# Linear attention and soft experts on one core: w's load moves to ScalarE's queue, the second expert product takes 384 columns at once, the last weight piece has one row

## Chip, cores and metric

The kernel runs on one core of a Trainium2 chip. The core has a matrix engine (PE, TensorE), a vector engine (DVE), a scalar engine (ACT), a general one (POOL, GpSimd), a sequencer that here only issues transfers (SP), and 16 DMA engines, which carry every transfer, whoever issues it. The metric is the device time of one execution, in microseconds (us); it is the median of several runs. The time before is 122.52 us, the median of three runs (122.45 to 122.78).

## What is computed

Two parts follow one another. First a recurrent linear attention with a decay `w` and a bonus `u` per head; then its output, seen as 3072 tokens of 384, goes through eight soft experts.

```python
batch, n_heads, seq, head_dim = (4, 8, 768, 48)     # r, k, v; w and u are (8, 48)
N, D, E, S_per_e, F = (3072, 384, 8, 4, 1024)       # phi (384, 32), w1 (8, 384, 1024), w2 (8, 1024, 384)

for t in range(S):                                   # attention, state is D x D for each head
    cur = einsum('bhd,bhe->bhde', u[None] * kt, vt)
    y[:, :, t] = einsum('bhd,bhde->bhe', rt, state + cur)
    state = w[None, :, :, None] * state + einsum('bhd,bhe->bhde', kt, vt)
...
logits = x @ phi
d = exp(logits - logits.max(0)); d /= d.sum(0) + 1e-09       # over tokens
slot_input = d.T @ x                                         # 32 slots, 4 for each expert
for e in range(E):
    h = maximum(slot_input[e] @ w1[e], 0.0)
    slot_out[e] = h @ w2[e]
c = exp(logits - logits.max(1)); c /= c.sum(1) + 1e-09       # over slots
out = c @ slot_out
```

All inputs and the output are float32. The inputs r, k and v are 4.7 MB each, w1 and w2 together 25 MB, the output 4.7 MB.

## The kernel before

**Order.** Every instruction is recorded through a helper that keeps the order of the program on its engine, so each engine runs its instructions exactly as they are written; what is left to the framework are the waits between engines and the space in memory. The framework puts a wait wherever one instruction needs what another wrote, or writes where another still reads. Transfers that SP and ACT issue share eight completion semaphores in turn, so such a transfer also waits until an earlier holder of its semaphore has landed.

**Start.** SP issues w as one row of 384 numbers (`w_row`, line 105), then k, r and v of batch 0, two heads at a time, then batches 1 and 2 and phi. ACT loads its function table (line 106) and issues two small transfers of w and u into `wu` (107, 108). PE runs four warm-up matmuls (line 144), then spreads `w_row` over the 128 partitions (line 177); ACT takes the logarithm (178), DVE multiplies by positions (188), ACT exponentiates (192), and with these powers of w, called W, k and r are scaled into `kr` (228): on DVE for the first pair of heads, on POOL for all others.

**Attention.** The sequence of each pair of heads is cut into two halves of three chunks of 128 steps; one half is one step i of the main loop (32 steps, with some steps ahead of it to fill the pipeline). PE transposes `kr`, makes the chunk products, and ACT and DVE move results out of PSUM. At step 3 SP issues batch 3 of k, r and v into the buffer that batch 0 used. Phi is turned to bfloat16 (`phi_b`, line 558) at step 5 and rearranged by PE at step 6. From step 13 on POOL issues the weights, each expert's matrix as one transfer that also turns float32 to bfloat16 (`load_w`, lines 135 and 138): eight of w1 and then eight of w2, these into buffers of k, r and v that are free by then. Ahead of the first of them POOL copies one column of batch 3's k (line 571). The last matrix, w2 of expert 7, comes in three pieces, of 4, 2 and 2 of its 8 rows `y` (line 576); a row is 128 partitions by 384 columns.

**Dispatch.** `acc` (32 slots by three blocks, and the sums) collects the slot inputs over the chunks; it is first written when the first half of batch 0 is done.

**Experts.** The slots of four experts share the 128 partitions, 32 for each, so there are two groups g of four. After w1 (line 623) and the transposes (648) comes `second` (660): for each row y, each half x of the 384 columns and each expert j, one matmul of 192 columns onto the partitions of that expert. Half 0 is summed in PSUM bank Xb, half 1 in bank Yb. Group 1 is run as experts 4 and 5, then 6, then 7, each as its weights arrive. Then `so`, the slot outputs in bfloat16, is written by DVE (half 0, line 671) and by ACT (half 1, line 672), both scaled by `csr`.

**Output.** 24 tiles of 128 tokens. For each, PE multiplies the weights of the slots with `so` (line 684), DVE or ACT scales the result into an output buffer (686, 688), and SP or POOL sends the buffers off in groups of 1, 1, 2, 2, 2, 4, 4, 4 and 4 tiles (line 704). The first two tiles are done in halves, left half on DVE, right half on ACT; the six PSUM banks used in turn are T1, T0, Ab, Vb, Xb, Yb.

Of the kernel before, what the change touches and what calls it, by code (L numbers as in the profile page):

```python
# [9 lines left out]
def kernel(  # L10
# [16 lines left out]
    Nn, Dm = out.shape  # L27
    ES = moe_phi.shape[1]
    E = moe_w1.shape[0]
    F = moe_w1.shape[2]  # L30
    Spe = ES // E
    nM = Dm // C
    nF = F // C
# [13 lines left out]
    bf = mybir.dt.bfloat16  # L47
    i32 = mybir.dt.int32
    AF = mybir.ActivationFunctionType
    ALU = mybir.AluOpType  # L50

    def O(ins):
        return tc.keep_in_program_order(ins)

    pe, dve, act, pool, sp = nc.tensor, nc.vector, nc.scalar, nc.gpsimd, nc.sync

    big = ctx.enter_context(tc.tile_pool(name="big", bufs=1))
    cst = ctx.enter_context(tc.tile_pool(name="cst", bufs=1))
# [6 lines left out]
    EG = E // 2  # L65
# [4 lines left out]
    def w2_of(e):  # L70
        g, j = divmod(e, EG)
        return raw[1 + g][:].bitcast(bf)[:, j * eW2:(j + 1) * eW2].rearrange("p (y d) -> p y d", y=nF)

    def raw_of(which, b):
        return raw[b % NR][:, which * RW:(which + 1) * RW]
# [5 lines left out]
    Yb = psb.tile([128, 512], f32, name="Yb")  # L81
    Xb = psb.tile([128, 512], f32, name="Xb")
# [12 lines left out]
    w_row = early[0:1, 0:H * D]  # L95
# [5 lines left out]
    phi_f = late[:, 128:128 + nM * ES]  # L101
    wu = cst.tile([8, 128], f32, name="wu")
    wu3 = wu[:].rearrange("q (e s) -> q e s", s=64)
    O(dve.memset(wu[:], 1.0))
    O(sp.dma_start(out=w_row, in_=w.rearrange("(o h) d -> o (h d)", o=1)))
    O(act.preload_act_table_set("natural_log_exp_and_others"))
    O(act.dma_start(out=wu3[0:4, :, 0:D], in_=w.rearrange("(q e) d -> q e d", e=2)))
    O(act.dma_start(out=wu3[4:8, :, 0:D], in_=u.rearrange("(q e) d -> q e d", e=2)))
# [104 lines left out]
    ones = cst.tile([128, 128], bf, name="ones")  # L213
    Le_t = [cst.tile([128, L, 128], bf, name=f"Le{j}") for j in range(2)]
    phi_s = cst.tile([128, nM, ES], bf, name="phi_s")
    phi_b = cst.tile([128, nM * ES], bf, name="phi_b")
    assert JV == nM
    acc = cst.tile([128, NA], f32, name="acc")
    guard = cst.tile([128, 1], f32, name="guard")
    st = {}  # L220

# [70 lines left out]
    def a_pe(i):  # L292
        m, b, q, g, n = at(i)
        kT, rT = st["kT", m], st["rT", m]
        for c in range(L):
            t = slice((g * L + c) * C, (g * L + c + 1) * C)
            for e in range(2):
                s = slice(64 * e, 64 * e + 64)
                O(pe.matmul(Ab[:, e, c * C:(c + 1) * C], kT[s, t], rT[s, t]))  # L299

    def mask_f(i):
        AT = wk.tile([128, 2, L, C], bf, name="AT", bufs=2)
        st["AT", i] = AT
        O(dve.tensor_mul(AT[:], Ab[:, :, 0:T].rearrange("p e (c t) -> p e c t", c=L),  # L304
                         mask_ut[:, None, None, :].to_broadcast([128, 2, L, C])))
# [112 lines left out]
    def disp(n, ds_p, first=True):  # L418
        x, Le = st["x", n], st["Le", n]
        for mi in range(nM):  # L420
            for c in range(L):
                O(pe.matmul(ds_p[:, mi * ES:(mi + 1) * ES].rearrange("p (j x) -> p j x", j=EG), x[:, c, mi:Dm:nM],
                            Le[:, c, :].rearrange("p (j x) -> p j x", x=32)[:, :, 0:2 * Spe],
                            start=(first and mi == 0 and c == 0), stop=(c == L - 1), skip_group_check=True))
        for c in range(L):
            O(pe.matmul(ds_p[:, NA - 1:NA], Le[:, c, :], ones[:, 0:1],
                        start=False, stop=(c == L - 1), skip_group_check=True))

    def disp_ev(n, ds_p):
        if n == 0:  # L430
            O(dve.tensor_copy(acc[:], ds_p))
        else:
            O(dve.tensor_add(acc[:], acc[:], ds_p))
# [37 lines left out]
    Wf = [t[:].rearrange("p q j d -> p (q j d)") for t in W]  # L471
# [3 lines left out]
    def turn(n, blocks, bank, eng):  # L475
        x, w_ = st["x", n], L * len(blocks) * C
        for b, mi in enumerate(blocks):
            for c in range(L):
                o = (b * L + c) * C
                O(pe.transpose(bank[:, o:o + C], x[:, c, mi * C:(mi + 1) * C], ident[:]))  # L480
        dst = xs[:, n - n0, blocks[0]:blocks[-1] + 1].rearrange("p m c t -> p (m c t)")
        if eng is dve:
            O(dve.tensor_copy(dst, bank[:, 0:w_]))
        else:
            O(act.copy(dst, bank[:, 0:w_]))
# [8 lines left out]
    for i in range(-5, nH):  # L494
        mu, odd = divmod(i, 2)
        if 0 <= i + 1 < nH:
            a_pe(i + 1)
            mask_f(i + 1)
        if pend:
            disp_ev(*pend.pop())  # L500
        if i == nH - 1:
            turn(n0, (2,), Vb[:].bitcast(bf), act)
            disp(n0 - 1, ds_t)
            le_t(n0 - 1)
            let_ev(n0 - 1, None, dve)
        if 0 <= i < nH:
            y_pe(i)
            y_evac(i)
        if 0 <= i + 2 < nH:
            v_pe(i + 2)  # L510
            v_evac(i + 2)
        if 0 <= i + 1 < nH:
            m_pe(i + 1)
            z_evac(i + 1)
        if odd == 0 and 0 <= mu + 1 < nU:
            prod_f(mu + 1)
        if odd and i > 0 and mu + 2 < nU:
            b_pe(mu + 2)
            b_evac(mu + 2)
        if odd and 0 <= mu + 3 < nU:  # L520
            scale(mu + 3, 0)
        if not odd and 0 <= mu + 2 < nU:
            scale(mu + 2, 1)
        route(i, 0)
        if 0 <= mu + 2 < nU:
            t_pe(mu + 2, odd)
            route(i, 1)
            t_evac(mu + 2, odd)
            if odd and i < 0:
                b_pe(mu + 2)  # L530
                b_evac(mu + 2)
        else:
            route(i, 1)
        if odd == 0 and 0 <= mu + 2 < nU:
            v_cast(mu + 2)
        route(i, 2)
        if i == nH - 3:
            turn(n0, (0, 1), T0, act)
        if i == nH - 2:
            turn(n1, (0, 1), T1, act)  # L540
        for f, j, q in T_AT.get(i, ()):
            f(j, q)
        if i in (-4, -3):
            wu_steps(i + 4)
        if i in Z_AT:
            q = Z_AT[i]
            O(act.activation(out=zt[:, q, 2, :], in_=zt[:, q, 0, :], func=AF.Copy, scale=wT[:, q:q + 1]))
        if i == 2:
            O(pool.memset(ones[:], 1.0))
            for t in Le_t:  # L550
                O(pool.memset(t[:], 0.0))
        if i == 3:
            load_kr(0, k, B - 1, 0, H)
            load_kr(1, r, B - 1, 0, H)
            for h0 in range(0, H, 2):
                load_v(B - 1, h0, h0 + 2)
        if i == 5:
            O(act.copy(phi_b[:], phi_f))
        if i == 6:
            for mi in range(nM):  # L560
                for j in range(nM):
                    o = C * mi - j + nM - 1
                    O(pe.matmul(Xb[:, mi * ES:(mi + 1) * ES].rearrange("p (j g s) -> p j g s", g=2, s=Spe),
                                Q3[:, o:o + C],
                                phi_b[:, j * ES:(j + 1) * ES].rearrange("p (g j s) -> p j g s", g=2, s=Spe),
                                start=(j == 0), stop=(j == nM - 1)))
            O(act.copy(phi_s[:].rearrange("p m s -> p (m s)"), Xb[:, 0:nM * ES]))
        if i == 28:
            O(pool.memset(uns, 0.0))
        if i == min(W_AT):  # L570
            O(pool.tensor_copy(guard[:], raw_of(0, B - 1)[:, 0:1]))
        for _ in range(W_AT.get(i, 0)):
            load_w(nw)
            nw += 1
    assert nw == 2 * E - 1
    for y0, y1 in ((0, 4), (4, 6), (6, 8)):
        load_w(nw, y0, y1)


# [29 lines left out]
    csr = cst.tile([128, 1], f32, name="csr")  # L609
# [8 lines left out]
    hT = [Wf[1].bitcast(bf)[:, g * F:(g + 1) * F].rearrange("p (y c) -> p y c", c=C) for g in range(2)]  # L618
    for g in range(2):
        for a in range(2):  # L620
            for mi in range(nM):
                for j in range(EG):
                    O(pe.matmul(hb[g][a][32 * j:32 * j + 32, 0:FH], uns[:, mi, g, j, :],
                                w1_all[:, g * EG + j, mi, a * FH:(a + 1) * FH],
                                start=(mi == 0), stop=(mi == nM - 1), skip_group_check=True))
# [17 lines left out]
    HD = Dm // 2  # L643
# [7 lines left out]
        if g == 0:  # L651
            row_sums(0, 8)
    row_recip(0, 8)
    SO = [Xb[:, 0:HD], Yb[:, 0:HD]]

    def second(g, experts):
        for y in range(nF):
            for x in range(2):
                for j in experts:
                    O(pe.matmul(SO[x][32 * j:32 * j + 32, :], hT[g][:, y, 32 * j:32 * j + 32],  # L660
                                w2_of(g * EG + j)[:, y, x * HD:(x + 1) * HD],
                                start=(g == 0 and y == 0), stop=(g == 1 and y == nF - 1), skip_group_check=True))

    second(0, range(EG))
    second(1, range(EG - 2))
# [1 line left out]
    second(1, (EG - 2,))  # L667
    second(1, (EG - 1,))
    row_sums(8, 12)
    so = cst.tile([128, Dm], bf, name="so")  # L670
    O(dve.tensor_scalar_mul(so[:, 0:HD], SO[0], csr[:, 0:1]))
    O(act.activation(out=so[:, HD:Dm], in_=SO[1], func=AF.Copy, scale=csr[:, 0:1]))
    row_recip(8, 12)

    out_v = out.rearrange("(p n) m -> p n m", n=nN)
# [59 lines left out]
```

The softmax here doesn't subtract the row's maximum and nothing guards it: scores larger than these inputs give would overflow.

## Time and profile before

| what | us |
|---|---|
| median of three runs | 122.52 |
| the profiled execution itself | 122.36 |
| its span, first to last instruction | 120.5 |
| PE busy in the span | 102.6 (85%) |
| DVE busy | 96.4 (80%) |
| ACT busy | 83.7 (69%) |
| POOL busy | 59.7 (50%) |
| transfers issued by SP (k, r, v, output), as a share of 16 DMA engines | 41.3% |
| transfers issued by POOL (weights, part of the output) | 55.5% |

The profile is of one execution. Its page gives the busy time of each engine, the span in 40 equal slices with the busy tenths of each engine and of the 16 DMA engines, the transfer queues, the chain of work that ended last, and the costliest groups of instructions with what ended the idle time before them. The trace behind it can be asked for instructions in order of time, for windows, and for the landing events of a transfer: there are 16 of these for a large transfer, one from each DMA engine, and only the last releases who waits for it. PEld is PE's loading of weights, and SPq, ACTq and POOLq are the engines' sequencers, which issue transfers. L105 is line 105.

### The profile page before, as it was taken

Reading aid. Unit: us, or ns where it says so; the run is one execution under the profiler, and the core shown is the slowest. Engines: PE = TensorE matmul, PEld = TensorE weight load, DVE = VectorE, ACT = ScalarE, POOL = GpSimd, SP = SyncE. Lnnn points to the kernel's source line nnn. Section 1 sums busy time; section 2 is a strip of 40 time slices with the busy share of each in tenths; the row PEclk is TensorE's granted clock in tenths of the full one; section 3 lists DMA queues with packets and bytes.
Section 4 is the critical chain, followed back from the end, with each engine's and each line's share of the span. In section 5 each row is a group of like instructions: output and inputs, shape, how many; then the busy total and the mean of one; then the engine's idle time right before and its main releaser. Section 6 shows DMA issues by size and latency. Waiting matters only on the chain.

```text
span 120.5 us, 4334 instructions
## 1 busy us (share of the span) xinstructions
PE 102.6 (85%) x1795; PEld 82.9 (69%) x1797; DVE 96.4 (80%) x187; ACT 83.7 (69%) x183; POOL 59.7 (50%) x70
## 2 busy tenths in 40 slices
PE   5996977799999999999999999999979996796000
PEld 1465866687887988898888898888866686583000
DVE  6899999999999999899999899999943510399000
ACT  4459769797978998888898988997963510299000
POOL 7349534599999999797677593101000000012000
PEclk9999999999999999999999999999999999999755
DMA  2999999999999999999999999999999998069992
GB/s 38 322 362 373 374 367 371 364 391 362 330 380 382 323 204 216 218 213 212 220 206 222 211 220 209 215 215 215 224 208 220 208 206 165 16 261 389 396 420 100
DMA packets 20925, 31.79 MB, mean 264 GB/s; under 512 B 1129, under 2 KB 18026, under 8 KB 20906
## 3 DMA queue, kind: packets, MB, share of 16 engines
q0 software_dynamic: 2960, 14.55, 55.5%
q1 hardware_dynamic: 17922, 16.96, 41.3%
q8 instruction: 14, 0.23, 0.7%
q14 instruction: 5, 0.04, 0.1%
q10 hardware_dynamic: 24, 0.00, 0.0%
HBM read 39.38 MB, written 4.72 MB: 366 GB/s over the span
## 4 chain that ended last, share of the span: by engine, by line
PE 37%; DMA 31%; DVE 15%; issue 6%; ACT 1%; POOL 1%; POOLq 0%; DVEq 0%; ACTq 0%
DMA raw<-in_moe_w_dram 31%; PE Vb L284 5%; PE T L235 4%; PE Ab L299 4%; PE Yb L352 3%; DVE W L188 3%; PE T L247 2%; PE Mb L325 2%; DVE prod L257 2%; PE Yb L365 2%; DVE kn L252 2%; DVE Z L341 2%; PE Xb L387 2%; PE Xb L380 2%; PE Yb L144 2%
## 5 line engine op out<-in xcount | busy, mean ns | idle before, releaser
L228 POOL TENSOR_TENSOR kr<-raw,W 128x576 bf16<-128x576 f32 x30 | 42.2, 1426 | 12.4 <-PE T L235 5.2
L304 DVE TENSOR_TENSOR AT<-Ab,mask_ut 128x768 bf16<-128x768 f32 x32 | 30.2, 945 | 0.8 <-PE Ab L299 0.6
L284 PE MATMUL Vb<-v_bf,Q 128*128 128x96 bf16 x288 | 18.2, 211 | 0.0
L235 PE MATMUL T<-ident,kr 128*128 128x128 bf16 x192 | 17.2, 230 | 1.0 <-POOL kr L228 1.0
L284 PEld LDWEIGHTS <-Q 128*128 128x128 bf16 x288 | 16.3, 100 | 1.5 <-issue 0.2
L241 ACT COPY kT<-T 128x768 bf16<-128x768 bf16 x16 | 12.8, 799 | 4.6 <-PE T L235 3.3
L241 ACT COPY rT<-T 128x768 bf16<-128x768 bf16 x16 | 12.8, 800 | 4.2 <-PE T L235 3.6
L257 DVE TENSOR_TENSOR prod<-T,kT 128x768 bf16<-128x768 bf16 x16 | 15.2, 947 | 0.0
L342 DVE TENSOR_TENSOR dv<-vn,Mb 128x288 bf16<-128x288 bf16 x32 | 14.1, 440 | 0.0
L235 PEld LDWEIGHTS <-kr 128*128 128x128 bf16 x192 | 12.7, 102 | 1.8 <-POOL kr L228 1.2
L290 ACT CAST vn<-Vb 128x288 bf16<-128x288 f32 x32 | 13.4, 419 | 0.1
L372 ACT CAST x<-Yb 128x288 bf16<-128x288 f32 x32 | 13.1, 409 | 0.2 <-PE Yb L365 0.2
L341 DVE TENSOR_TENSOR Z<-Mb,zt 128x288 bf16<-128x288 f32 (+1 forms) x32 | 12.7, 395 | 0.6
L299 PE MATMUL Ab<-rT,kT 64*128 64x128 bf16 x192 | 11.1, 222 | 2.1 <-DVE AT L304 2.1
L704 POOL DMA_DIRECT2D out_dram<-W x1 | 0.5, 549 | 24.9 <-DVE W L686 24.9
L325 PE MATMUL Mb<-vn,kn 128*128 128x96 bf16 (+2 forms) x80 | 11.5, 242 | 0.0
L352 PE MATMUL Yb<-vn,AT 128*128 128x48 bf16 x192 | 10.3, 185 | 0.1
L270 ACT CAST v_bf<-raw 128x576 bf16<-128x576 f32 x15 | 10.2, 677 | 0.0
L299 PEld LDWEIGHTS <-kT 64*128 64x128 bf16 x192 | 5.6, 95 | 5.6 <-DVE AT L304 2.0
L138 POOL DMA_DIRECT2D raw<-in_moe_w_dram x10 | 5.5, 557 | 7.9 <-DMA raw<-in_moe_w_dram 6.5
L352 PEld LDWEIGHTS <-AT 128*128 128x128 bf16 x192 | 7.1, 96 | 3.3
L365 PE MATMUL Yb<-dv,ident 128*128 128x288 bf16 x32 | 9.1, 285 | 0.2
(143 smaller groups left out, 221.7 us busy)
## 6 DMA issues: line engine op xcount, KB each, us to landing
w_all<-in_moe_w_dram POOLq DMA_DIRECT2D x8, 768.0 KB, 12.7
raw<-in_moe_w_dram POOLq DMA_DIRECT2D x7, 768.0 KB, 18.4
raw<-in_v_dram SPq DMA_DIRECT2D x12, 288.0 KB, 6.2
raw<-in_k_dram SPq DMA_DIRECT2D x8, 288.0 KB, 6.1
raw<-in_r_dram SPq DMA_DIRECT2D x8, 288.0 KB, 5.9
raw<-in_k_dram SPq DMA_DIRECT2D x2, 1152.0 KB, 12.9
raw<-in_r_dram SPq DMA_DIRECT2D x2, 1152.0 KB, 10.3
out_dram<-raw POOLq DMA_DIRECT2D x2, 768.0 KB, 6.8
```

The source lines that it names most:

```text
L228: O(eng.tensor_mul(kr[:, j].rearrange("p j (h s) -> p j h s", s=64)[:, :, :, 0:D], src, W[j][:, q].rearrange("p j (h d) -> p j h d", h=2)))
L235: O(pe.transpose(bank[:, x * C:(x + 1) * C], kr[:, j, x, :], ident[:]))
L241: O(act.copy(t[:].rearrange("p (s j) -> p s j", j=J), bank[:, 0:S].rearrange("p (j s) -> p s j", j=J)))
L257: O(dve.tensor_mul(pr[:].rearrange("p (s j) -> p s j", j=J), T1[:, 0:S].rearrange("p (j s) -> p s j", j=J), st["kT", m][:].rearrange("p (s ...
L284: O(pe.matmul(Vb[:, c * P2:(c + 1) * P2], Q3[:, o:o + C], vb[:, :, g, j, :], start=(j == 0), stop=(j == JV - 1)))
L290: O(act.copy(vn[:].rearrange("p c e d -> p (c e d)"), Vb[:, 0:L * P2]))
L299: O(pe.matmul(Ab[:, e, c * C:(c + 1) * C], kT[s, t], rT[s, t]))
L304: O(dve.tensor_mul(AT[:], Ab[:, :, 0:T].rearrange("p e (c t) -> p e c t", c=L), mask_ut[:, None, None, :].to_broadcast([128, 2, L, C])))
L325: O(pe.matmul(o, kn[:, g * L + c, :], vc, start=first, stop=True, skip_group_check=True))
L341: O(dve.tensor_mul(Z[:], Mb[:, 0:x * P2].rearrange("p (c e) -> p c e", c=x), zt[:, q, 0:x, :]))
L342: O(dve.tensor_mul(dv[:], st["v", i][:].rearrange("p c e d -> p (c e) d"), Mb[:, 288:288 + 2 * L, None].to_broadcast([128, L * 2, D])))
L352: O(pe.matmul(Yb[:, o:o + D], AT[:, e, c, :], vn[:, c, e, :], start=first, stop=False, skip_group_check=True))
```

## The change

Five edits:

1. `w_row` is issued by ACT ahead of its table load, not by SP; the first transfer of SP is now the first k.
2. `phi_b` has no tile of its own; it lies in the space of `acc`.
3. The pieces of the last weight matrix are of 4, 3 and 1 rows, not 4, 2 and 2.
4. `second` makes one matmul of 384 columns in place of two of 192, and both halves are summed in bank Xb. PE has 64 matmuls and 64 weight loads less: 3461 rows in its program, not 3589.
5. `so` has no tile of its own; it lies in the second W buffer, behind the slot inputs. DVE and ACT write its halves from bank Xb both.

```diff
-    O(sp.dma_start(out=w_row, in_=w.rearrange("(o h) d -> o (h d)", o=1)))
+    O(act.dma_start(out=w_row, in_=w.rearrange("(o h) d -> o (h d)", o=1)))
     O(act.preload_act_table_set("natural_log_exp_and_others"))
...
-    phi_b = cst.tile([128, nM * ES], bf, name="phi_b")
     acc = cst.tile([128, NA], f32, name="acc")
+    phi_b = acc[:].bitcast(bf)[:, 0:nM * ES]
...
-    for y0, y1 in ((0, 4), (4, 6), (6, 8)):
+    for y0, y1 in ((0, 4), (4, 7), (7, 8)):
         load_w(nw, y0, y1)
...
-    SO = [Xb[:, 0:HD], Yb[:, 0:HD]]
+    SO = Xb[:, 0:Dm]
     def second(g, experts):
         for y in range(nF):
-            for x in range(2):
-                for j in experts:
-                    O(pe.matmul(SO[x][32 * j:32 * j + 32, :], hT[g][:, y, 32 * j:32 * j + 32],
-                                w2_of(g * EG + j)[:, y, x * HD:(x + 1) * HD],
-                                start=(g == 0 and y == 0), stop=(g == 1 and y == nF - 1), skip_group_check=True))
+            for j in experts:
+                O(pe.matmul(SO[32 * j:32 * j + 32, :], hT[g][:, y, 32 * j:32 * j + 32],
+                            w2_of(g * EG + j)[:, y, :],
+                            start=(g == 0 and y == 0), stop=(g == 1 and y == nF - 1), skip_group_check=True))
...
-    so = cst.tile([128, Dm], bf, name="so")
-    O(dve.tensor_scalar_mul(so[:, 0:HD], SO[0], csr[:, 0:1]))
-    O(act.activation(out=so[:, HD:Dm], in_=SO[1], func=AF.Copy, scale=csr[:, 0:1]))
+    so = Wf[1].bitcast(bf)[:, 2 * F + nM * ES * 8:2 * F + nM * ES * 8 + Dm]
+    O(dve.tensor_scalar_mul(so[:, 0:HD], SO[:, 0:HD], csr[:, 0:1]))
+    O(act.activation(out=so[:, HD:Dm], in_=SO[:, HD:Dm], func=AF.Copy, scale=csr[:, 0:1]))
```

More of the change, by code (lines that the diff above doesn't have):

```diff
@@ L557 @@
         if i == 5:
-            O(act.copy(phi_b[:], phi_f))
+            O(act.copy(phi_b, phi_f))
         if i == 6:
```

## Prediction

> **What bounds the kernel now.** I read the page's forty slices first, then windows over the seams between stages, then the order of time at the start and at the end. The two lines of the DMA engines in the slices:
>
> ```profile
> DMA  2999999999999999999999999999999998069992
> GB/s 38 322 362 373 374 367 371 364 391 362 330 380 382 323 204 216 218 213 212 220 206 222 211 220 209 215 215 215 224 208 220 208 206 165 16 261 389 396 420 100
> ```
>
> The engines of the core (PE, DVE) look busy, but the transfer engines are full from 3 us to 101 us and again from 106 us to 118 us. There are three streams: k, r and v at some 370 GB/s, the expert weights at some 215 GB/s, the output at some 400 GB/s. Between the second and the third lies the one gap, at 101 to 106 us. The seams, in windows of the trace (width, then busy us of PE, PEld, DVE, ACT, POOL, then clock, DMA share, GB/s):
>
> ```profile
> 3.00:40.00 37.00, 33.68 (x516) 26.33 (x516) 36.62 (x66) 28.98 (x62) 26.79 (x23) 1.00 1.09 365
> 42.00:43.00 1.00, 0.98 (x21) 0.78 (x19) 1.00 (x3) 1.00 (x4) 0.98 (x3) 1.00 0.84 181
> 43.00:101.00 58.00, 56.34 (x1164) 47.63 (x1163) 47.58 (x94) 44.09 (x101) 26.16 (x29) 1.00 1.04 214
> 102.00:103.00 1.00, 0.82 (x9) 0.68 (x9) 0.00 (x0) 0.00 (x0) 0.00 (x0) 1.00 0.34 60
> 107.00:118.00 11.00, 3.43 (x21) 2.25 (x19) 4.68 (x10) 4.27 (x9) 1.61 (x3) 0.78 1.00 401
> ```
>
> A share of 1.0 means that nothing is waiting to be issued: a stream ends earlier only if it starts earlier. So I price each edit by what it does to the start of the first stream, to the hand-over at 42 us, and to the gap between the last weight and the first output. Compute inside 43 to 99 us doesn't count: the matmuls of w2 sit waiting for weights from 99.4 us on.
>
> **Start: k first.** The order of time (start, duration, both in us):
>
> ```profile
> 0.73 1.28 ACT L106 ACT_TABLE_LOAD   x1 [0.73 <-PEq L719]
> 0.74 0.34 SPq L105 DMA_DIRECT2D LexpT<-in_w_dram  x1
> 1.01 1.24 ACTq L107 DMA_DIRECT2D wu<-in_w_dram  x1
> 1.14 0.41 SPq L115 DMA_DIRECT2D raw<-in_k_dram  x1
> ...
> 3.13 0.50 PEld L177 LDWEIGHTS Xb<-LexpT 1*128 1x128 f32 x2 [0.84 <-DVE sk L164]
> ...
> 40.22 0.75 POOL L135 DMA_DIRECT2D w_all<-in_moe_w_dram  x1
> ```
>
> Taking w off SP's queue moves the first k from 1.14 to 0.74, 0.40 us, and with it all of k, r and v (SP's later rows keep pace with the drain, so they follow). ACT now issues three transfers, not two: its table load ends some 0.34 later, at 2.35, and the two wu transfers shift by as much. Cover: ACT's first computation is at 3.91, and wu (landed at 5.68 by the landing records) is first read at 7.70. w itself landed at 2.04, and the matmul that spreads it (L177) starts at 3.13 behind four warm-up matmuls: 1.1 us of slack.
>
> How much of the 0.40 reaches the end? The first weight transfer is issued at 40.22, in POOL's own order behind a row of scalings that hang on DVE and ACT, not on these loads; that doesn't move. Its 16 landings, one from each DMA engine, come at 46.31 to 47.16. Nine lie within 0.2 of the first: those engines had done with v and are bound by POOL's issue. Seven lie 0.36 to 0.85 later: they still had v to move, and are bound by the first stream. Fourteen transfers later the spread is 97.69 to 99.55, and its steps can be read as the old lag plus 0.97 for each block of instructions that an engine also fetched:
>
> ```profile
> q8 instruction: 14, 0.23, 0.7%
> ```
>
> These are 14 packets of 16 KB, 0.9 to 1.1 us each. Three engines have lag 1.83 to 1.86 (0.85+0.97), one has 1.42 (0.44+0.97). That last one gets one more block at 99.56 and so finishes everything last, at 103.79; the three others finish at 103.28 to 103.34. Its first lag, 0.44, is of the kind that k's start sets, and can shrink by 0.40 at most, to the floor that POOL sets about 0.1 above the earliest. I take a gain of 0.35. Bounds: 0.40, and 0.00 if it is POOL that holds this engine. If ACT's issue at the same moment holds up SP's for as long as w's whole issue (0.34), 0.06 is left.
>
> **End: one bank, and one row in the last piece.** The end of the weights and the first output:
>
> ```profile
> 103.83 0.24 PE L660 MATMUL Xb<-raw,W 128*32 128x192 bf16 x1 [0.41 <-DMA raw<-in_moe_w_dram]
> ...
> 104.08 0.24 PE L660 MATMUL Yb<-raw,W 128*32 128x192 bf16 x1
> ...
> 104.28 0.42 DVE L671 TENSOR_SCALAR so<-Xb,csr 128x192 bf16<-128x192 f32 x1 [7.27 <-PE Xb L660]
> 104.36 0.42 ACT L672 ACTIVATE so<-Yb,csr 128x192 bf16<-128x192 f32 x1 [7.53 <-PE Yb L660]
> ...
> 104.75 0.33 PE L684 MATMUL T<-so,LexpT 128*128 128x192 bf16 x2
> ...
> 105.11 0.42 ACT L688 ACTIVATE raw<-T,rsr 128x192 f32<-128x192 f32 x1 [0.33 <-PE T L684]
> ...
> 105.56 0.84 SPq L704 DMA_DIRECT2D out_dram<-raw  x2
> ```
>
> The bytes of the last two pieces are the same, 192+192 KB against 288+96 KB. A packet of 1536 B comes every 0.1165 us on an engine and one of 3072 B every 0.2295, so the fixed part is 0.004 and the sum is unchanged: the last landing stays. The piece before it lands about 0.49 ahead of it (8 packets of 768 B, 0.060 each) instead of 0.95, and its three rows need three matmuls of 0.165 (the step of a 384-column matmul at L684): just done when the last row arrives. After the last landing one matmul of 384 columns remains (0.33, as at L684) in place of four steps of 0.083 and an end: it ends at 104.16, not at 104.24 (Xb) and 104.33 (Yb). That is a gain of 0.08 for DVE's half and 0.17 for ACT's. The 64 matmuls and 64 weight loads that vanish lie under the wait for weights: nothing.
>
> Now the price. Both halves of `so` are read from one PSUM bank. In the changed program as built, ACT's half no longer waits for PE, it waits for DVE's half. DVE: 104.16+0.04 = 104.20, to 104.62. ACT: 0.033 later (DVE to ACT in this trace: 30 to 34 ns), 104.65 to 105.07. PE's second product for the first output tile, with its sequencer order behind the first, starts 0.05 later at 105.12; before it was 104.78+0.05 = 104.83. So +0.29. Queued behind it on PE are all further output products, and on ACT the first tile's right half (105.11, now 105.40), which SP's first output transfer waits for. Later rows can't buy it back: the third stream is full from its first packet on. Bounds: +0.29, less at most 0.1 of small holes in that stream; −0.08 if the two reads ran side by side.
>
> The Trainium skill, "PSUM — Partial Sum Buffer", section "PSUM bank collisions raise a hardware error", speaks against the edit: ScalarE and VectorE must not read one bank in the same quadrant at the same time, disjoint columns included. The rows above overlap by 0.34 us, but in two banks, so no run here shows the rule itself; by it the end costs +0.29, without it −0.08.
>
> The two tiles that move into others (`phi_b` into `acc`, `so` into the tail of W) add no wait that binds: `acc` is first written several steps after `phi_b` was read, and that part of W is free.
>
> **Sum.** −0.35 + 0.29 = −0.06. The profiled execution took 122.36 (span 120.5 and 1.86 around it), giving 122.30; it stands 0.16 under the median of 122.52, so for the median I say 122.46. Two real effects that nearly cancel.
>
> **Rivals.**
> - *w arrives late (slower).* On ACT's queue w now travels beside k's packets. Nearest rows: alone it landed 0.96 after its issue ended; the two wu transfers, under load, 1.8 and 2.75. From 1.08 the latter gives 3.83, 0.70 after L177 wants it. DVE is busy without a break until 27 us, so POOL's issue at 40.22 would slip by 0.70 too, and the floor of the first weight landing goes to 47.01 or a little over: the last engine comes 0.28 later instead of 0.35 sooner. With the end, +0.57: 123.09. It decides from a landing at 3.13. Against it: w's packet (1.66) is ahead of k's first (now about 1.79). Chance 0.12.
> - *The late block of instructions falls on another engine.* On one of the three late ones: 103.34−0.40+0.97 = 103.91, +0.12, with the end +0.41: 122.93, chance 0.12. On an early one: the three late ones end the stream at 102.94, −0.85, with the end −0.56: 121.96, chance 0.12. For it: PE's instructions change. Against: only 128 fewer, all in the last stage, so earlier blocks are fetched as before.
> - *The start's gain stops at POOL* (the weights don't end earlier): +0.29, 122.81, chance 0.06.
> - *The change doesn't do what it says*: the two halves are read side by side after all: −0.35−0.08 = −0.43, 122.09, chance 0.06.
>
> **How the numbers follow.** The forecast keeps 0.52, with its own range 122.2 to 122.75 from the bounds of its two terms. A measurement of this kernel can tell some 0.3%, 0.37 us, from no change: faster is under 122.15, slower over 122.89. Faster: 0.12 (early engine) + 0.05 (side by side) + 0.02 (forecast's edge) = 0.19. Slower: 0.12 (w late) + 0.09 (late engine) + 0.02 (POOL) + 0.02 = 0.25. Same: 0.56. A range of 122.0 to 123.0 leaves out the greater part of the two outer cases, under 0.2.
>
> **What would show it.** Right: first k at 0.74; L177 still at 3.13; POOL's first weight issue still at 40.2; the first weights' last landing some 0.4 earlier and the last matmul of w2 starting near 103.5; then ACT's half of `so` starting 0.03 after DVE's ends, and 0.29 more than before from the last landing to SP's first output transfer. Wrong: L177 or POOL's issue later (w), the last landing not moved (POOL or another block), or the two halves overlapping.

## Result and profile after

The changed kernel takes 122.84 us (median of four runs, 122.74 to 122.93), the kernel before in the same series 122.65 (122.45 to 122.83). The ratio is 1.0016, 95% interval [0.9995, 1.0036]: no measurable change. The profiled execution took 122.84 with a span of 121.02; before it was 122.36 with 120.53.

The slices of the page of the changed kernel, and the row of its instruction blocks:

```profile
DMA  3999999999999999999999999999999997069992
GB/s 88 297 346 374 374 375 365 371 390 359 334 369 379 304 206 219 211 219 211 219 217 207 217 215 215 218 211 218 213 219 215 217 203 141 4 256 386 402 414 102
...
q8 instruction: 13, 0.21, 0.7%
```

A slice is 3.0 us. The first has 88 GB/s where it had 38: k did start earlier. The second has 297 instead of 322, the third 346 instead of 362: the lead melts in the 6 us after it was won. The gap between the weights and the output (digits 7 and 0, before 8 and 0) stands where it stood. The order of time of the changed kernel at the start (start and duration in us):

```profile
0.74 0.44 SPq L115 DMA_DIRECT2D raw<-in_k_dram  x1
0.74 0.53 ACTq L105 DMA_DIRECT2D LexpT<-in_w_dram  x1
...
1.30 1.28 ACT L106 ACT_TABLE_LOAD   x1 [1.30 <-PEq L718]
...
3.13 0.50 PEld L177 LDWEIGHTS Xb<-LexpT 1*128 1x128 f32 x2 [0.84 <-DVE sk L164]
...
40.24 0.75 POOL L135 DMA_DIRECT2D w_all<-in_moe_w_dram  x1
```

First k at 0.74, L177 at 3.13 and POOL's first weight issue at 40.24 (was 40.22) are as forecast. But the landing records have the last of k, r and v at 43.86 (before 43.67), the first weights on the 16 engines at 46.29 to 47.34 (46.31 to 47.16), and the last weight at 103.94 (103.79). In this pair of executions nothing ended earlier. The end, in the order of time:

```profile
103.53 0.81 PE L659 MATMUL Xb<-raw,W 128*32 128x384 bf16 x4 [0.64 <-DMA raw<-in_moe_w_dram]
...
104.38 0.42 DVE L670 TENSOR_SCALAR W<-Xb,csr 128x192 bf16<-128x192 f32 x1 [7.35 <-PE Xb L659]
...
104.83 0.42 ACT L671 ACTIVATE W<-Xb,csr 128x192 bf16<-128x192 f32 x1 [7.98 <-DVE W L670]
104.85 0.24 PE L683 MATMUL T<-W,LexpT 128*128 128x192 bf16 x1
...
105.31 0.24 PE L683 MATMUL T<-W,LexpT 128*128 128x192 bf16 x1 [0.21 <-ACT W L671]
...
106.03 0.84 SPq L703 DMA_DIRECT2D out_dram<-raw  x2
```

The halves of `so`, side by side before (104.28 and 104.36), now follow one another (104.38, 104.83). The two output products of the first tile, a pair before ("x2" at 104.75, the second of them at 104.83), are apart, and the second one waits for ACT. Per profiled execution: last weight landing to the start of that product is 1.37 (105.31−103.94) against 1.04; first output issue 106.03 against 105.56. Of the 0.48 between the two executions, 0.33 is the end and 0.15 the later last landing.

How much is that 0.15 worth? The ten kernels profiled below that issue the weights in the same place (these two among them) have their last landing at 103.79 to 104.36, mean 104.04: a scatter of 0.57. So 0.15 between two single executions says nothing, and the parts were run alone.

### The profile page after: what moved, and what is told of

The parts are those of the page before. It is cut to its first block, busy times and chain, and to the rows that moved or that the text cites. A ratio compares the mean times of both kernels' runs of the same rounds, so it can differ in the third digit from the quotient of the medians.

```text
span 121.0 us, 4208 instructions
## 1 busy us (share of the span) xinstructions
PE 101.7 (84%) x1733; PEld 79.7 (66%) x1733; DVE 96.5 (80%) x187; ACT 83.5 (69%) x183; POOL 59.5 (49%) x70
## 4 chain that ended last, share of the span: by engine, by line
PE 48%; DMA 21%; DVE 12%; ACT 5%; issue 3%; POOL 1%; POOLq 0%
DMA raw<-in_moe_w_dram 21%; PE Vb L284 7%; PE T L235 7%; PE Ab L299 5%; PE Yb L352 4%; PE Yb L144 3%; PE Mb L325 3%; PE T L247 3%; DVE AT L304 3%; PE Yb L365 2%; DVE prod L257 2%; PE Xb L387 2%; PE Xb L380 2%; PE Yb L363 2%; DVE W L188 2%
## 5 line engine op out<-in xcount | busy, mean ns | idle before, releaser
L235 PE MATMUL T<-ident,kr 128*128 128x128 bf16 x192 | 16.6, 224 | 1.3 <-POOL kr L228 1.3
L284 PE MATMUL Vb<-v_bf,Q 128*128 128x96 bf16 x288 | 17.5, 206 | 0.0
L284 PEld LDWEIGHTS <-Q 128*128 128x128 bf16 x288 | 15.8, 98 | 1.6
L235 PEld LDWEIGHTS <-kr 128*128 128x128 bf16 x192 | 12.2, 100 | 2.0 <-POOL kr L228 1.4
```

The costliest lines, as they stand in the source:

```text
L235: O(pe.transpose(bank[:, x * C:(x + 1) * C], kr[:, j, x, :], ident[:]))
L284: O(pe.matmul(Vb[:, c * P2:(c + 1) * P2], Q3[:, o:o + C], vb[:, :, g, j, :], start=(j == 0), stop=(j == JV - 1)))
```

## Experiments

In the diffs, `-` is the kernel before and `+` the experiment, unless it is said that the changed kernel is the base. Times are medians, with the kernel before beside them from the same series.

**The start alone.**

```diff
-    O(sp.dma_start(out=w_row, in_=w.rearrange("(o h) d -> o (h d)", o=1)))
+    O(act.dma_start(out=w_row, in_=w.rearrange("(o h) d -> o (h d)", o=1)))
```

> The kernel before with one edit: w is issued by ACT, so k goes first on SP. Theory A (the 0.40 us is lost within the first 8 us, in slow packets of the first v and k, and POOL's issue holds the weights): first k at 0.74, but the last landing of k, r and v within 0.2 us of the 43.67 of the kernel before, first output transfer within 0.2 us of 105.56 apart from chance in the last weight landing, ratio 0.998 to 1.001. Theory B (the gain of the start reaches the end, as predicted): last landing of k, r and v near 43.3, last weight landing near 103.4, ratio near 0.997.

122.56 against 122.63, ratio 1.0000 [0.9983, 1.0016]: −0.21 to +0.20 us, which excludes the 0.35. Last k/r/v landing 43.72, last weight landing 104.04. The window 4 to 5 us (width, busy us of PE, PEld, DVE, ACT, POOL, clock, DMA share, GB/s) shows where the lead goes; first the kernel before, then this one, then the changed kernel:

```profile
4.00:5.00 1.00, 1.00 (x3) 0.18 (x3) 0.99 (x4) 0.24 (x2) 0.09 (x1) 1.00 1.06 330
```

```profile
4.00:5.00 1.00, 1.00 (x3) 0.18 (x3) 1.00 (x4) 0.24 (x2) 0.14 (x1) 1.00 0.81 151
```

```profile
4.00:5.00 1.00, 1.00 (x3) 0.19 (x3) 0.99 (x4) 0.24 (x2) 0.10 (x1) 1.00 0.81 187
```

All three have a slow patch there, against some 370 GB/s later. In this microsecond it is deeper with w on ACT's queue: the mean of five kernels is 196 GB/s, of five with w on SP 277. Added up from the packet records, the five with w on ACT have moved 0.446 MB by 3.5 us, the five with w on SP 0.300: a lead of 0.146 MB, or 0.39 us at 370 GB/s, just the 0.40 of the earlier issue. By 9 us it is 2.153 against 2.132 MB: 0.06 us is left. (With one further kernel of each kind, the last one and the one with less of v, 0.12 is left; the standard error of either figure is 0.06 to 0.07.)

After that the lead doesn't shrink further: it is within 0.03 us of these values at 20 us. The last landing of k, r and v can't tell 0.35: in four kernels each it lies at 43.48 to 43.86 with w on ACT and at 43.67 to 44.30 with w on SP. The two latest of these, the end alone and the bank alone, fall behind between 30 and 35 us, not at the start.

A DMA share near 1.0 doesn't tell how many bytes move. The window 4 to 5 us of the kernel with one engine for both halves and of the one with the end alone, both described below:

```profile
4.00:5.00 1.00, 1.00 (x3) 0.19 (x3) 1.00 (x4) 0.24 (x2) 0.14 (x1) 1.00 0.92 204
```

```profile
4.00:5.00 1.00, 1.00 (x3) 0.17 (x3) 1.00 (x4) 0.24 (x2) 0.13 (x1) 1.00 0.91 270
```

The shares are alike, the bytes differ by a third.

**The end alone, then its two parts.** The first is the changed kernel with w back on SP:

```diff
-    O(act.dma_start(out=w_row, in_=w.rearrange("(o h) d -> o (h d)", o=1)))
+    O(sp.dma_start(out=w_row, in_=w.rearrange("(o h) d -> o (h d)", o=1)))
```

> The changed kernel with w back on SP's queue. Theory A (the bank costs 0.3 us whatever the start does, and the start gave next to nothing): from the last weight landing to the second half product of the first output tile 1.33 to 1.40 us, against 1.04 before; ratio to the kernel before 1.002 to 1.004, the same as the changed kernel within 0.001. Theory B (the start gained 0.3 us and the end costs 0.5): ratio 1.004 to 1.006.

122.86 against 122.63, 1.0028 [1.0011, 1.0045]; 1.33 from last landing (103.84) to the second output product. Next, the kernel before with the new pieces, its two banks kept:

```diff
-    for y0, y1 in ((0, 4), (4, 6), (6, 8)):
+    for y0, y1 in ((0, 4), (4, 7), (7, 8)):
```

> The kernel before with the last weight pieces of 4, 3 and 1 rows, matmuls of 192 columns in two banks as before. Theory A: the last landing doesn't depend on the pieces; after it two steps of 0.083 remain in place of four, so DVE's half of so begins 0.17 us sooner after the last landing (0.32 in place of 0.49) and the ratio is 0.998 to 0.9995. Rival C (a piece of one row costs time of its own, in packets of 768 bytes): the last landing comes 0.2 us or more later against the other engines' landings, ratio 1.000 to 1.002.

122.47, 0.9988 [0.997, 1.0005]. Its end:

```profile
104.27 0.42 DVE L671 TENSOR_SCALAR so<-Xb,csr 128x192 bf16<-128x192 f32 x1 [6.79 <-PE Xb L660]
104.35 0.42 ACT L672 ACTIVATE so<-Yb,csr 128x192 bf16<-128x192 f32 x1 [7.04 <-PE Yb L660]
...
104.74 0.33 PE L684 MATMUL T<-so,LexpT 128*128 128x192 bf16 x2
```

The halves overlap by 0.34 again and the products are a pair. The last landing was 103.92, so DVE starts 0.35 behind it (before: 0.49) and the second product 0.90 behind it: the piece alone gains 0.14. Third, the single bank with the old pieces (base: changed kernel, w on SP):

```diff
-    O(act.dma_start(out=w_row, in_=w.rearrange("(o h) d -> o (h d)", o=1)))
+    O(sp.dma_start(out=w_row, in_=w.rearrange("(o h) d -> o (h d)", o=1)))
...
-    for y0, y1 in ((0, 4), (4, 7), (7, 8)):
+    for y0, y1 in ((0, 4), (4, 6), (6, 8)):
```

> The changed kernel with w on SP's queue and the pieces of 4, 2 and 2 rows: only the product of 384 columns in one bank is left (and the two tiles that lie in others). Theory A: after the last landing two matmuls of 384 columns (0.165 and 0.33), then DVE's half, then ACT's half behind it: second half product about 1.50 us after the last landing, ratio 1.003 to 1.005. Rival C (the piece costs, not the bank): ratio 0.999 to 1.001.

123.12, 1.0041 [1.0023, 1.0058]: of the three edits run alone (w's queue, the pieces, the bank) the one whose interval lies clear of 1. Its end:

```profile
104.91 0.42 DVE L670 TENSOR_SCALAR W<-Xb,csr 128x192 bf16<-128x192 f32 x1 [7.88 <-PE Xb L659]
...
105.36 0.42 ACT L671 ACTIVATE W<-Xb,csr 128x192 bf16<-128x192 f32 x1 [8.51 <-DVE W L670]
...
105.83 0.24 PE L683 MATMUL T<-W,LexpT 128*128 128x192 bf16 x1 [0.21 <-ACT W L671]
```

From the last landing (104.34) to the second product it is 1.49: the bank costs 0.45, the time by which ACT starts behind DVE. 0.45 − 0.14 = 0.31, and the changed kernel shows 0.33, the end alone 0.29. This run also has `so` in W, so W could be what ties the two engines together. It isn't: in the program as built, ACT's half waits for DVE also when `so` is a tile of its own, and it waits for PE again when the products go to two banks and `so` stays in W. And the kernel before has ACT and DVE write two parts of that same W buffer side by side, from the two banks Ab and Vb:

```profile
96.24 0.58 ACT L649 COPY W<-Ab 128x512 bf16<-128x512 bf16 x1 [0.43 <-PE Ab L648]
...
96.47 0.42 DVE L650 COPY W<-Vb 128x512 bf16<-128x512 bf16 x1 [0.46 <-PE Vb L648]
```

The wait is one that the framework puts into the program; no run shows what the chip would do without it.

**One engine for both halves** (base: changed kernel).

```diff
-    O(dve.tensor_scalar_mul(so[:, 0:HD], SO[:, 0:HD], csr[:, 0:1]))
-    O(act.activation(out=so[:, HD:Dm], in_=SO[:, HD:Dm], func=AF.Copy, scale=csr[:, 0:1]))
+    O(dve.tensor_scalar_mul(so, SO, csr[:, 0:1]))
```

> The changed kernel, but DVE alone writes all 384 columns of so in one instruction; ACT reads nothing from that bank. Theory A (the price is ACT's half waiting behind DVE's): DVE's instruction takes about 0.60, the second half product comes 1.13 to 1.20 us after the last weight landing in place of 1.33 to 1.36, ratio to the kernel before 1.0005 to 1.002. Rival (the price is in the matmul of 384 columns or in the shared tile): still 1.30 or more, ratio 1.002 to 1.004.

122.86 against 122.66, 1.0020 [1.0001, 1.0039].

```profile
104.80 0.62 DVE L670 TENSOR_SCALAR W<-Xb,csr 128x384 bf16<-128x384 f32 x1 [7.45 <-PE Xb L659]
105.47 0.33 PE L682 MATMUL T<-W,LexpT 128*128 128x192 bf16 x2 [0.34 <-DVE W L670]
...
106.28 0.84 SPq L702 DMA_DIRECT2D out_dram<-raw  x2
```

One instruction of 0.62 replaces 0.42 + 0.03 + 0.42; the second product starts 1.18 behind the last landing (104.36). The first output issue is 1.92 behind it, against 2.09 in the changed kernel and 1.77 before. With one bank, one engine is the shorter way by 0.17 in the traces (the times, 122.86 and 122.84, don't tell them apart); two banks are shorter still.

**A shorter first stream.** If an earlier end of k, r and v were worth its time, then leaving a load out would show it. Here the last load of v (heads 6 and 7 of batch 3) is not issued:

```diff
-            for h0 in range(0, H, 2):
+            for h0 in range(0, H - 2, 2):
                 load_v(B - 1, h0, h0 + 2)
```

> The kernel before, with the last v load of batch 3 (288 KB, 0.78 us of the first stream) left out: heads 6 and 7 of batch 3 read old values. It asks what an earlier end of the first stream is worth at all. Theory A (POOL's issue of the first weights at 40.22 holds the weights): first stream's last landing near 42.9, first weights' last landing 46.4 to 46.7 in place of 47.16 to 47.83, last weight landing 0.0 to 0.5 earlier than the mean of 103.97 of the four kernels with w on SP, ratio 0.997 to 1.000. Theory B (the weights end as much earlier as the first stream does): last weight landing near 103.2, ratio 0.993 to 0.995.

122.63 against 122.66, 1.0001 [0.9984, 1.0017]. The last landing of k, r and v is 43.11, 0.56 earlier than before. The window at the hand-over:

```profile
42.00:43.00 1.00, 0.98 (x21) 0.78 (x18) 1.00 (x3) 1.00 (x4) 0.98 (x3) 1.00 0.65 137
```

The share of the DMA engines falls from 0.84 to 0.65. One such microsecond scatters (the changed kernel has 0.64 there with all of v), but over 40 to 44 us the share is 0.93 at 205 GB/s where the kernel before has 1.07 at 257 and the changed kernel 1.08 at 256. So 0.21 of the 0.29 MB that were left out were not replaced by weights in these 4 us: most of what the first stream gave up was idled away, since POOL issued the first weight at 40.25 as ever. The last weight landed at 103.95. The first weights' latest landing, 47.31, did not come down towards the earliest (46.25) either, so the latest engine, which the prediction put down to the late v, is not set by the first stream. The others may be in part: four engines, not seven, are 0.36 or more behind the earliest.

**The weights one step earlier.** The kernel before with one entry of the list of steps moved (from step 16 on the counts agree):

```diff
-    W_AT = {13: 1, 14: 1, 15: 1, 16: 1, 18: 1, 19: 1, 20: 1, 22: 1, 23: 1, 25: 1, 26: 5}
+    W_AT = {12: 1, 13: 1, 14: 1, 15: 1, 18: 1, 19: 1, 20: 1, 22: 1, 23: 1, 25: 1, 26: 5}
```

> The kernel before, with the first weight transfer one step earlier in POOL's order (steps 12, 13, 14, 15 and 18 in place of 13, 14, 15, 16 and 18; the rest as before). Theory A (POOL's issue at 40.22 holds the weights, and DMA engines wait for it at 41 to 43 us): first weight issue near 38.8, no window at 41 to 44 us with a DMA share under 0.95, first stream's end up to 1 us later as it shares, last weight landing 103.0 to 103.7 in place of 103.8 to 104.4, ratio 0.993 to 0.998. Rival (the weights are held by their own rate, and the early issue only delays v): last weight landing as before, ratio 0.999 to 1.001.

121.97 against 122.54, 0.9949 [0.9923, 0.9975].

```profile
39.03 0.75 POOL L135 DMA_DIRECT2D w_all<-in_moe_w_dram  x1
...
42.00:43.00 1.00, 0.98 (x21) 0.78 (x17) 1.00 (x2) 1.00 (x3) 1.00 (x1) 1.00 1.12 258
```

POOL issues 1.2 earlier, the share at the hand-over is 1.12, and the last weight lands at 103.40. It is POOL that held the second stream.

**The same with w on ACT** (on the kernel before).

```diff
-    O(sp.dma_start(out=w_row, in_=w.rearrange("(o h) d -> o (h d)", o=1)))
+    O(act.dma_start(out=w_row, in_=w.rearrange("(o h) d -> o (h d)", o=1)))
...
-    W_AT = {13: 1, 14: 1, 15: 1, 16: 1, 18: 1, 19: 1, 20: 1, 22: 1, 23: 1, 25: 1, 26: 5}
+    W_AT = {12: 1, 13: 1, 14: 1, 15: 1, 18: 1, 19: 1, 20: 1, 22: 1, 23: 1, 25: 1, 26: 5}
```

> The kernel before with the first weight one step earlier and w on ACT, pieces of 4, 2 and 2 rows: does k's early start count once POOL no longer holds the weights? Theory A (it does, by what is left of the 0.40 after the first 8 us, 0.1 to 0.2): ratio 0.992 to 0.9945, under the 0.9949 of the early weights alone, last weight landing 103.0 to 103.4. Rival (it gives nothing there either; the step from 0.9949 to 0.9907 was the piece and chance): ratio 0.9945 to 0.9965.

122.08 against 122.78, 0.9947 [0.9924, 0.997], the ratio of the earlier weights alone; last landing 103.78. So no gain of the earlier k is seen with the hand-over moved either. Alone this run would not exclude one: between two ratios from two series the uncertainty is some 0.0035, or 0.43 us. That little of the lead reaches the hand-over is shown by the moved bytes (0.06 to 0.12 us at 9 us). The hand-over was also not the same in the two kernels: the first stream's last packets end at 53.30 here, one every 0.49 us between those of the weights, against 43.32 with the weights moved alone.

**What slows the first microseconds?** Two guesses, one execution each. In the kernel before, the third load is v, whose packets are smaller; so batch 0 was loaded as k, r, k, r, v, v:

```diff
-    load_batch(0, 2)
+    for h0 in (0, 4):
+        load_kr(0, k, 0, h0, h0 + 2)
+        load_kr(1, r, 0, h0, h0 + 2)
+        load_kr(0, k, 0, h0 + 2, h0 + 4)
+        load_kr(1, r, 0, h0 + 2, h0 + 4)
+        load_v(0, h0, h0 + 2)
+        load_v(0, h0 + 2, h0 + 4)
```

> The kernel before with the loads of batch 0 in another order: two pairs of k and r first, then two of v, so v's first packets come 1.5 us later. Theory D (the slow patch at 4 to 6 us is met by the first packets of v, whenever they come): 360 GB/s or more until about 5.8, then the slow patch. Theory E (the small transfers of wu at 3.3 to 5.9, or something else at a fixed time, slow the stream): the patch stays at 4.2 to 6.0 with k's and r's packets in it.

Time 122.86. The patch is there again at 4.1 to 4.2 us, now in k's packets, a little shallower (the others with w on SP have 244 to 330 GB/s in the first of these two windows):

```profile
4.00:5.00 1.00, 1.00 (x3) 0.18 (x3) 0.99 (x4) 0.24 (x2) 0.10 (x1) 1.00 1.05 332
5.00:6.00 1.00, 1.00 (x3) 0.30 (x2) 0.69 (x2) 1.00 (x3) 0.00 (x0) 1.00 1.05 316
```

Then the two transfers into `wu`, from ACT's queue to SP's, behind batch 0's loads:

```diff
-    O(act.dma_start(out=wu3[0:4, :, 0:D], in_=w.rearrange("(q e) d -> q e d", e=2)))
-    O(act.dma_start(out=wu3[4:8, :, 0:D], in_=u.rearrange("(q e) d -> q e d", e=2)))
...
     load_batch(0, 2)
+    O(sp.dma_start(out=wu3[0:4, :, 0:D], in_=w.rearrange("(q e) d -> q e d", e=2)))
+    O(sp.dma_start(out=wu3[4:8, :, 0:D], in_=u.rearrange("(q e) d -> q e d", e=2)))
```

> The kernel before with the two small transfers of wu issued by SP behind batch 0, so that PE's and ACT's first use of wu comes some 6 us later; the time itself is not the point. Theory E (the small transfers slow the first stream at 4 to 6 us): 360 GB/s or more from 4.2 to 6.0. Rival F (they don't; the patch comes with the third load, whatever it is): rates of 220 to 330 GB/s there as before.

Time 126.96: PE now waits 6.1 us for `wu` at 13.9 instead of 7.7, and with it ACT and POOL. But the first 6 us answer the question:

```profile
4.00:5.00 1.00, 1.00 (x3) 0.19 (x3) 0.98 (x4) 0.24 (x2) 0.09 (x1) 1.00 1.00 267
5.00:6.00 1.00, 1.00 (x3) 0.30 (x2) 0.68 (x2) 1.00 (x3) 0.00 (x0) 1.00 0.99 286
```

The patch is there without any transfer of ACT's. Neither guess can be the whole cause, and the cause stays open.

**What is left of the change, and a faster kernel.** First the start and the pieces with two banks (on the kernel before):

```diff
-    O(sp.dma_start(out=w_row, in_=w.rearrange("(o h) d -> o (h d)", o=1)))
+    O(act.dma_start(out=w_row, in_=w.rearrange("(o h) d -> o (h d)", o=1)))
...
-    for y0, y1 in ((0, 4), (4, 6), (6, 8)):
+    for y0, y1 in ((0, 4), (4, 7), (7, 8)):
```

> The kernel before with w on ACT and pieces of 4, 3 and 1 rows, products of 192 columns in two banks: the change without its product of 384 columns. Theory A: second half product 0.88 to 0.92 us after the last weight landing, the start gives nothing, ratio 0.998 to 0.9995. Theory B (start gains too): ratio 0.995 to 0.997.

122.44 against 122.66, 0.9991 [0.9973, 1.001]: last landing 103.92, the second product 0.90 behind it, as with the pieces alone. Then the same with the weights one step earlier:

```diff
-    O(sp.dma_start(out=w_row, in_=w.rearrange("(o h) d -> o (h d)", o=1)))
+    O(act.dma_start(out=w_row, in_=w.rearrange("(o h) d -> o (h d)", o=1)))
...
-    W_AT = {13: 1, 14: 1, 15: 1, 16: 1, 18: 1, 19: 1, 20: 1, 22: 1, 23: 1, 25: 1, 26: 5}
+    W_AT = {12: 1, 13: 1, 14: 1, 15: 1, 18: 1, 19: 1, 20: 1, 22: 1, 23: 1, 25: 1, 26: 5}
...
-    for y0, y1 in ((0, 4), (4, 6), (6, 8)):
+    for y0, y1 in ((0, 4), (4, 7), (7, 8)):
```

> The same edit of POOL's order, with w on ACT and pieces of 4, 3 and 1 rows in two banks. Theory A: with the hand-over free of a hold, k's early start counts too, and the piece gives its 0.14: ratio 0.001 to 0.003 under that of the edit alone. Rival: 0.001 under it at most (the piece alone).

121.66 against 122.54, 0.9907 [0.9876, 0.9938], faster than both kernels: last landing 103.35, the second product 0.88 behind it. The product of the two ratios that it is made of, 0.9991 and 0.9949, is 0.9940, just above that interval; with the pieces alone (0.9988) it would be 0.9937, inside. The ratio is 0.0042 under that of the earlier weights alone, where 0.001 at most was expected of the piece and 0.001 to 0.003 if the start counted too. Of the 0.23 us between the two profiled executions (121.72 and 121.95), the end gives 0.16 (0.88 against 1.04) and the last landing 0.05 (103.35 against 103.40). This run has only six executions, and the one with the start and the earlier weights showed no such gain; whether the start has a part in the rest stays open.

## Why the prediction came out as it did

The forecast was no measurable change, and that is what was measured; but of its two terms only one is real. That the time came out inside the range is luck in part: without the start's −0.35 the same sum gives 122.81, which is inside 122.0 to 123.0 as well, so the time alone doesn't tell the two accounts apart. The landings and the runs of the parts do.

- **Start, −0.35: the step that failed.** Right: first k at 0.74, w in time for L177, POOL's issue unmoved. Wrong: "a stream ends earlier only if it starts earlier" was used as if the converse held. A share near 1.0 counts busy DMA engines, not bytes: in the patch 0.92 went with 204 GB/s in one kernel and 0.91 with 270 in another. The lead was won (0.39 us at 3.5 us) and lost (0.06 to 0.12 left at 9 us), and the start alone measured 1.0000, which excludes a gain of 0.35. The Trainium skill, "DMA: Bandwidth & Descriptors", section "Issuing engines are not separate DMA queues", says that transfers of all issuers interleave on the same 16 engines and that a second issuer saves only the issuing time. The rows agree as far as that goes: 0.40 us of issue was saved. What became of them the moved bytes show. The prediction's own sign of being wrong, a last landing that has not moved, is what came.
- **The seven late DMA engines** were read as bound by v. The shorter first stream ended 0.56 earlier and left the latest at 47.31 and the time at 1.0001. So the second half of the step, that such a lead would pass the hand-over, was wrong as well. The bound of 0.00 that I had kept "if it is POOL that holds this engine" is what came, and the rival "the start's gain stops at POOL", at 122.81, is nearest to the 122.84 measured. It was given 0.06, too little. Its mechanism was half of the truth: POOL does hold the second stream (moved, it gives 0.5%), but most of the lead is lost long before it gets there.
- **End, +0.29: right.** ACT's half starts 0.03 behind DVE's end, and the second output product 0.33 later behind the last landing than before. The term is 0.04 too small: by its working that product stood 1.33 behind the landing, and 1.37 was measured. DVE's half starts 0.44 behind the landing, not 0.41 (see the piece below), and the product 0.06 behind ACT's end, not 0.05. The parts run alone: single bank +0.45, last piece −0.14. The 0.33 passes to the output's issue (+0.47 with the 0.15 of the landing) and to the time.
- **The rule on PSUM banks** that the prediction weighed is still not shown by a run, since neither the kernel before nor the changed one reads one bank from ACT and DVE at once. What the wait in its place costs is shown: 0.45.
- **The piece's last landing**: piece (4,7) landed at 103.49, 0.45 ahead of the last, where 0.49 was worked out. Its three matmuls, 0.162 apart from 103.53, were therefore not quite done in time: the last row's matmul started at 104.02, 0.07 behind the landing, where it starts 0.04 behind it when it waits for the row (before: 103.83 and 103.79).
- **ACT's table load** went from 0.73 to 1.30 and ended at 2.58, not 2.35: an issue of 0.53 sits ahead of it. Its cover (first computation at 3.91) held. The transfers into `wu` were issued at 1.34 and 2.11 (before: 1.01 and 2.28), so only the first of them moved back.
- **Block on another engine**: the changed kernel fetched 13 blocks, not 14, and the last landing lies within the scatter of the others. The block that is missing is the last one, which the kernel before fetched at 104.04, behind the last landing; the one ahead of it is there in both (99.56 before, 99.25 after). No run moved a block by itself, so this rival was not tested.
- **w late, and halves side by side**: both fell, by L177 at 3.13 (w had landed at 2.38) and by ACT's wait for DVE.

So the medians' +0.19 fits the end alone (+0.29 to +0.33 by the traces, 1.0028 by its own run) with nothing from the start; the interval of the ratio, −0.06 to +0.44 us, holds it.

## What to carry to other kernels

In this kernel a full transfer stream that started earlier did not end the kernel earlier. To judge such an edit, ask whether bytes, not busy time, keep the lead, and whether the next stream is held by another engine's program order: count moved bytes at two points, and look at the seam, where a gain that can't be used appears as a falling DMA share. Before merging two accumulators into one PSUM bank, look at who evacuates them: here two engines that had worked side by side became a chain, by a wait that the framework put in, and 64 matmuls fewer under a wait for data paid nothing for it. When the last landing of a single execution scatters by more than the expected gain, run the parts alone and measure from the landing.

## What was not expected of the hardware

- In all kernels here transfers slow down at about 4 to 6 us: 151 to 332 GB/s in the window 4 to 5 us, with packets of 0.2 to 1.3 us where most take 0.03 to 0.05 later. In most kernels it begins close to the third load's first packets (with the pieces alone at 3.3 us, ahead of them), and in that window it is deeper when the loads begin 0.40 earlier beside w on ACT's queue. It is there with k's packets in v's place and without `wu`'s transfers.
- Leaving out a transfer that ends the first stream gave nothing (1.0001), while issuing the next stream's first transfer 1.2 us earlier, beside the still busy first one, gave 0.5%.
